# Sparse attention and a token mixer on one core: batch 0's theta and first mix half in plain float32, mixing weights split later, batch 0's scores from copied keys, and a new order

## The chip, the cores and the metric

The kernel runs on one core of a Trainium2 chip. The metric is the device time of one execution in microseconds (us), as the median of several runs. One further execution was recorded by the hardware profiler; durations come from that record.

The engines are named as in the profile: PE (TensorE, matrix products), PEld (its weight loads), DVE (VectorE), ACT (ScalarE), POOL (GpSimd) and SP (SyncE, which here issues all DMAs). Each engine works off its own list of instructions in a fixed order and waits where an operand is not there yet.

## The reference

Attention with a window and block sums, then a mixer over tokens and channels. Cut to what matters:

```python
# attention: B, H, S, D = 4, 8, 768, 64; block 32, window 16
k_sum = k.reshape(B, H, 24, 32, D).max(axis=3)
v_sum = v.reshape(B, H, 24, 32, D).mean(axis=3)
scores = concat(where(|i - j| < 16, q @ k.T / 8, -1e9), q @ k_sum.T / 8 + log(32))
x = softmax(scores) @ concat(v, v_sum)        # laid out as (B, S, 512)
# mixer
theta = x @ w_theta                           # 512 x 512
zr, zi = x * cos(theta), x * sin(theta)
u = x + w_tok_r @ zr + w_tok_i @ zi           # 768 x 768, over tokens
out = u + relu(u @ w_ch)                      # 512 x 512
```

The four mixer weights come to the device as float64-like 8-byte words and are turned into float32 there.

## The kernel before

**Tiles.** A batch has 768 tokens, in six tiles of 128; the whole run has 24 tiles. A tile goes through these steps, and the name in brackets is that of the step in the planner's tables:

- `att_tile` (KV, S, SM, AV): load queries and values, scores (L598, 118 keys for each group of 64 queries: 24 block maxima and 94 neighbours), masked minimum (L619, DVE), exponential (L623, ACT), transposes on PE (L632) with a copy out (L636), product with the values (L606), division (L651 on ACT or L653 on DVE).
- `turn_tile` (X): transpose the result `xn` on PE (L662). From it come `x` (kept for the sum), and the split into a rounded part `xh` and a rest `xl` (L446, L448 and L667).
- `theta_tile` (TH, Z): theta on PE (L686), range reduction (L694, L697, L698, L703), sine and cosine (ACT, L709 and L710, with table loads between exponential and sine), products with `xn` (L718), one for each half of the channels: the first half goes into `w`, the second into `zb`.
- `split_z` makes `zh` and `zl` of a half of the channels.
- `mix_step(b, h, s)` (M0, M1): for batch b, half h of the channels and token tile s, 4 groups of 6 products on PE (L739) into PSUM tiles `m`. After six steps a half is complete; `x` is added to it on DVE (L754) and it is sent to DRAM.

At the end the last matrix product (`out_unit`, L787) runs for all batches.

**Split products.** A product with full precision is made of three passes of the type float32r: rounded weight by rounded data, rest of the weight by rounded data, rounded weight by the rest of the data. So weights and data are split into a rounded part and a rest.

**Weights.** `load_f64` handles one block of a weight: four blocks of theta (`wth`, 128 x 512), twelve of the token mixer (`wt`, 128 x 768) and at the end four of the last product. Its steps are the DMA, the magnitude (L492 on ACT or L494 on DVE), clamp (L496), shift (L498), two assembling operations (L500, L502), the rounded part (L446 on ACT, L448 on DVE) and the rest (L455 on DVE or POOL). The split block takes the place of the 8-byte words in the same buffer. All sixteen blocks pass through here in the first 90 us of a run.

**Keys.** In batch 0 (`DIRECT=1` counts batches) the scores read the block maxima `ks` and the keys `kn` directly, as two products each. In the other batches ACT or POOL copy both into one tile `k` (L591), which has one buffer, and there is one product of 118 columns.

**Order.** Nothing runs in the order of the source. `Program` collects all operations with a cost for each engine that may take them, and plans the order of every engine ahead, with four rounds of forward and backward passes and a last pass in which the tables `OFF` (a shift of rank) and `HOLD` (an earliest time) for each step act. The emitted lists are fixed; on the chip only semaphores hold an instruction back.

## Time and profile before

| | |
|---|---|
| median of 3 runs | 486.13 us (486.02 to 486.48) |
| the profiled execution: its time, its span | 486.1 us, 484.3 us |
| instructions | 10093 |
| DMA | 62.13 MB, 128 GB/s over the span |
| PE, time busy in the first 108 us | 72.5 us |
| DVE, time busy from 12 to 96 us | 81.1 of 84 us |
| ACT, time busy from 24 to 120 us | 85.1 of 96 us |

The span runs from the first to the last instruction; 1.8 us of the execution's time lie around it. A row of a timeline gives the start, the length, the engine, the line, the operation, the tile written and those read, and a count where like rows are merged. Rows of one engine overlap by some hundredths of a microsecond, and by more on PE, where products are pipelined; so the spacing of starts is the price there, and the mean length is not. One float32 product (not float32r) appears as two PE records.

### The profile page before, as it was taken

The page shows a single profiled execution, that of the slowest core. Times are in us where ns is not written, and L with a number is a line of the kernel's source. Part 1 is how long each engine was busy: PE and PEld are TensorE (multiplying, and loading weights), DVE is VectorE, ACT ScalarE, POOL GpSimd, SP SyncE. Part 2 cuts the span into 40 slices and gives each one's busy share as a digit, 9 for nine tenths or more (in the row PEclk, how much of TensorE's full clock was granted, in tenths as well). Part 3 has the DMA queues.
Part 4 walks back from the last instruction along what each step waited for, and adds up shares of the span by engine and source line. Part 5 has one row for each costly group of instructions (what it writes and reads, how often), then busy time and mean ns, then how long its engine had stood idle before and what let it go on. Part 6 is the DMA issues. An engine that isn't in the chain of part 4 may idle for free.

```text
span 484.3 us, 10093 instructions
## 1 busy us (share of the span) xinstructions
PE 444.8 (92%) x3864; PEld 378.1 (78%) x3864; DVE 301.6 (62%) x871; ACT 302.3 (62%) x663; POOL 51.6 (11%) x85
## 2 busy tenths in 40 slices
PE   0856676899999999999999999999999999999997
PEld 0344555778888878888888888888888899999996
DVE  3999999987784755476665745542645691334343
ACT  1678979799987776678896879536644640031120
POOL 0003111410200010011021110101000100001010
PEclk9979799899999999999999999999999999999999
DMA  8996824454461341013511411020012440256553
GB/s 306 364 345 200 325 76 172 140 164 136 121 214 56 100 143 33 1 56 122 191 56 56 142 37 55 7 94 1 0 67 88 152 132 0 99 162 213 196 180 130
DMA packets 30768, 62.13 MB, mean 128 GB/s; under 512 B 3584, under 2 KB 14080, under 8 KB 30720
## 3 DMA queue, kind: packets, MB, share of 16 engines
q1 hardware_dynamic: 30720, 61.49, 38.6%
q8 instruction: 30, 0.49, 0.4%
q14 instruction: 18, 0.15, 0.1%
HBM read 48.90 MB, written 12.58 MB: 127 GB/s over the span
## 4 chain that ended last, share of the span: by engine, by line
PE 74%; DVE 14%; ACT 7%; issue 2%; DMA 2%; SPq 0%; POOL 0%; ACTq 0%; POOLq 0%
PE m L739 36%; PE c L787 14%; PE t L686 12%; PE pa L606 4%; PE pa L632 4%; PE s L598 3%; DVE f L500 2%; DVE f L502 2%; PE t L662 2%; DMA kn<-kT 2%; DVE wt L455 1%; ACT e L623 1%; ACT L709 1%; DVE f L496 1%; DVE ks L522 1%
## 5 line engine op out<-in xcount | busy, mean ns | idle before, releaser
L739 PE MATMUL m<-wt,zh 128*128 128x512 f32 (+1 forms) x768 | 169.5, 342 | 1.7 <-ACT zh L446 1.7
L739 PEld LDWEIGHTS m<-wt,zh 128*128 128x128 f32 x768 | 121.1, 189 | 20.6 <-ACT zh L446 2.1
L739 PE MATMUL m<-wt,zl 128*128 128x512 f32 (+1 forms) x384 | 99.1, 339 | 0.7 <-DVE zl L455 0.7
L686 PE MATMUL t<-wth,xh 128*128 128x512 f32 x192 | 66.8, 430 | 8.0 <-DVE xl L667 6.7
L739 PEld LDWEIGHTS m<-wt,zl 128*128 128x128 f32 x384 | 58.6, 188 | 9.3 <-DVE zl L455 1.0
L787 PE MATMUL c<-cuh,wth 128*128 128x384 f32 x256 | 65.2, 335 | 0.0
L623 ACT ACTIVATE e<-e,st 128x118 f32<-128x118 f32 x192 | 60.1, 386 | 5.1 <-DVE st L619 4.9
L619 DVE CUSTOM_DVE_ANT_0 e<-s,cs 128x118 f32<-128x118 f32 x192 | 42.2, 273 | 20.1 <-PE s L598 15.8
L446 ACT CAST cuh<-cu 128x384 fp32r<-128x384 f32 x32 | 16.0, 513 | 60.2 <-DMA cu<-u_scratch 60.1
L787 PEld LDWEIGHTS c<-cuh,wth 128*128 128x128 f32 x256 | 45.8, 188 | 0.4
L792 DVE SCALAR_TENSOR_TENSOR cu<-c,cu 128x384 f32<-128x384 f32 x32 | 17.1, 554 | 43.6 <-PE c L787 43.5
L686 PEld LDWEIGHTS t<-wth,xh 128*128 128x128 f32 x192 | 31.4, 196 | 14.9 <-DVE xl L667 8.1
L787 PE MATMUL c<-cul,wth 128*128 128x384 f32 x128 | 43.0, 336 | 0.0
L686 PE MATMUL t<-wth,xl 128*128 128x512 f32 x96 | 39.4, 410 | 0.0
L697 DVE TENSOR_SCALAR w<-w 128x512 f32<-128x512 f32 x19 | 8.1, 426 | 46.0 <-ACT w L694 46.0
L632 PE MATMUL pa<-cs,e 128*118 128x128 f32 x192 | 29.7, 281 | 6.7 <-ACT xn L651 5.2
L636 ACT COPY e<-pa 118x512 f32<-118x512 f32 x45 | 25.2, 584 | 13.3 <-PE pa L632 13.3
L632 PEld LDWEIGHTS pa<-cs,e 128*118 128x118 f32 x192 | 23.1, 139 | 12.7 <-ACT xn L651 6.3
L606 PEld LDWEIGHTS pa<-v,e 118*64 118x64 f32 x768 | 24.6, 137 | 9.2 <-ACT e L636 5.3
L694 ACT ACTIVATE w<-t,bmagic 128x512 f32<-128x512 f32 x24 | 16.5, 687 | 24.1 <-PE t L686 23.6
L606 PE MATMUL pa<-v,e 118*64 118x65 f32 x768 | 28.2, 224 | 3.6 <-ACT e L636 3.6
L591 POOL COPY k<-kn 128x188 f32<-128x188 f32 x40 | 14.6, 392 | 118.2 <-PE s L598 98.8
(81 smaller groups left out, 657.3 us busy)
## 6 DMA issues: line engine op xcount, KB each, us to landing
v<-vg SPq DMA_DIRECT2D x48, 195.0 KB, 2.9
q<-qg SPq DMA_DIRECT2D x24, 256.0 KB, 3.4
cu<-u_scratch SPq DMA_DIRECT2D x32, 192.0 KB, 3.0
out<-cu SPq DMA_DIRECT2D x32, 192.0 KB, 1.9
kn<-kT SPq DMA_DIRECT2D x6, 798.0 KB, 6.5
wt<-wtr SPq DMA_DIRECT2D x6, 768.0 KB, 10.8
wt<-wti SPq DMA_DIRECT2D x6, 768.0 KB, 9.8
f<-vT SPq DMA_DIRECT2D x12, 384.0 KB, 3.2
```

The costliest lines, as they stand in the source:

```text
L446: nc.scalar.copy(dst(), src())
L591: lambda e, dst=dst, src=src: (nc.scalar.copy if e == "ACT" else V[e].tensor_copy)(dst(), src()), rd, [(k, key)], due, port=BOTH)
L606: mm(2 * 0.433, [lambda n=n, g=g, a=a: nc.tensor.matmul(xa[a].get()[ROW[g], n], turned[a].get()[:NK, n * P + g * QT:n * P + (g + 1) * QT], ...
L619: op({"DVE": 0.205}, lambda eng, n=n: nc.vector.tensor_tensor_reduce(e()[:, n], sc[n % 2].get()[:, 2 * a + n // 2], mask(m), -SCALE, 3.0e3 ...
L623: op({"ACT": 0.288}, lambda eng, n=n: nc.scalar.activation(e()[:, n], e()[:, n], AF.Exp, bias=st.get()[:, n:n + 1], scale=-1.0), [(st, n)] ...
L632: mm(NH * 0.109, [lambda n=n: nc.tensor.transpose(tp.get()[:NK, n], e()[:, n], ident()) for n in range(NH)], [e_ref, (cs, "ident")], [tp], ...
L636: lambda e: (nc.scalar.copy if e == "ACT" else nc.vector.tensor_copy)(t.get()[:NK], tp.get()[:NK].rearrange("k n q -> k (n q)")), [tp], [t ...
L686: calls = [lambda t=t, xx=xx, k=k, c=c: nc.tensor.matmul(th.get(), xx.get()[:, c], w_th[c].get()[:, k], start=(c == 0 and t == 0), stop=(c ...
L694: op({"ACT": 0.59}, lambda e: nc.scalar.activation(r(), th.get(), AF.Identity, bias=bmagic.get(), scale=1.0 / TWO_PI), [th, bmagic], [R], due)
L739: nc.tensor.matmul(acc[th](), zz.get()[:, r, cc], w_t[s, r].get()[:, k, TT[th]], start=(s == 0 and r == 0 and t == 0 and (th == 0 or c == 0)),
L787: calls = [lambda t=t, k=k, uu=uu, c=c, co=co, acc=acc: nc.tensor.matmul(acc.get(), w_ch[c].get()[:, k, co * P:(co + 1) * P], uu.get()[:, ...
L792: op({"DVE": c_dve(HT)}, lambda e, co=co, acc=acc: nc.vector.scalar_tensor_tensor(u.get()[:, co], acc.get(), 0.0, u.get()[:, co], ALU.max, ...
```

## The change

The diff of the tables is of no use to a reader: `OFF` and `HOLD` are replaced as a whole, and the three numbers of the planner's last pass with them. What it does to the order is shown below. The rest, cut to its core:

```diff
+def c_raw(n):
+    return n * 1.675e-3
...
-            A1=13, T1=10, PREP=5, QB=2, VSPE=1, VB=4, KN=2, DIRECT=1, XA=6, ...
+            A1=13, T1=10, PREP=5, QB=2, VSPE=1, VB=4, KN=2, DIRECT=0, RT=6, RM=6, XA=6, ...
...
-        op({"ACT": c_act(n), "DVE": c_dve(n)}, magnitude, [raw], [f_ref], due)
+        op({"ACT": c_act(n), "DVE": c_dve(n, "fast")}, magnitude, [raw], [f_ref], due, port=BOTH)
...
-        hi_op(lambda: w.get()[:, 0], f, n, [f_ref], [(w, 0)], due)
-        lo_op(lambda: w.get()[:, 1], f, lambda: w.get()[:, 0], n, [f_ref, (w, 0)], [(w, 1)], due)
+        return (to, f_ref if into is None else key)
+
+    def split_f64(j, tag, whole, n, due, pool=wpool, bufs=1):
+        pr.late, pr.key = K["R_W2"], ("W2", j)
+        src, key = whole
+        w = tag if isinstance(tag, Ref) else Ref(pool, [P, 2, n], F32R, tag=tag, bufs=bufs)
+        hi_op(lambda: w.get()[:, 0], src, n, [key], [(w, 0)], due, engines=("ACT", "DVE", "POOL"))
+        lo_op(lambda: w.get()[:, 1], src, lambda: w.get()[:, 0], n, [key, (w, 0)], [(w, 1)], due)
         return w
...
-        if b < K["DIRECT"]:
+        if b * NT + i < K["DIRECT"]:
...
+        if b * NT + i >= K["RT"]:
             x_h = Ref(tpool, [P, NC, P], F32R, tag="xh", bufs=K["XHB"])
             x_l = Ref(tpool, [P, NC, P], F32R, tag="xl", bufs=K["XHB"])
...
+            if b * NT + i < K["RT"]:
+                mm(c_raw(DM), [lambda c=c: nc.tensor.matmul(
+                    th.get(), xt[b].get()[:, c, i * P:(i + 1) * P], f_th[c][0](), start=(c == 0), stop=(c == NC - 1))],
+                   [(xt[b], i), f_th[c][1]], [th], due)
+                continue
...
-        split_z(b, 0, i, w, lambda: w.get()[:, :, :HC], due)
+        if not raw:
+            split_z(b, 0, i, w, lambda: w.get()[:, :, :HC], due)
+        else:
+            zs[b, 0, i] = z_0, None
...
+                if z_l is None:
+                    terms = ((z_h, f_t[2 * s + r][0]()),)
+                else:
+                    terms = [(zz, w_t[s, r].get()[:, k]) for zz, k in ((z_h, 0), (z_h, 1), (z_l, 0))]
...
+    def split_wt(j, f):
+        if len(slots) >= 2 * NT and f[1] and f[1][0] is slots[-2 * NT]:
+            f_ref = Ref(apool, [P, S], tag="f", bufs=K["FB"])
+            hi_op(f_ref.get, f[0], S, [f[1]], [f_ref], 1e6, engines=("ACT", "DVE", "POOL"))
+            f = f_ref.get, f_ref
+        w_t[j // 2, j % 2] = split_f64(NC + j, slot([P, 2, S], F32R), f, S, 1e6)
...
         mix_step(b, h, s, m_time(t))
+        if t < K["RM"]:
+            for j in (2 * s, 2 * s + 1):
+                split_wt(j, f_t[j])
```

In words:

- `RT=6`: theta of tiles 0 to 5 is one float32 product for each of its four blocks, of the unsplit `x` and the unsplit weight, in the place of three float32r products. `xh` and `xl` are not made for these tiles. The unsplit theta weights lie in the buffers of `xh` and `xl`.
  The split theta blocks, needed from tile 6 on, are made in the new order while the mixing blocks are assembled: two of the four subtractions on DVE, two on POOL.
- `RM=6`: the six steps of batch 0's first half (M0) take the unsplit product `zh` and the unsplit mixing weight, one float32 product where there were three. `zl` is not made for them.
- The twelve mixing blocks share one ring of twelve buffers. A block is split (rounded part, rest) after it has been assembled, under a rank of its own (W2). The rounded part may go to POOL too. One block, whose own buffer is the one to be written, is first copied. The DMA of the twelfth block waits for the buffer of the first.
- `DIRECT=0`: batch 0's scores use copied keys as the other batches do.

**Three places in the order.** Tile names carry a number where they would be mistaken otherwise. On DVE, the seventh and eighth mixing block of before (`f` is the float32 block in the making, `wt` the 8-byte words and later the split block, `e`, `st` belong to the scores):

```order
L498 TENSOR_SCALAR f<-f 128x768
L500 SCALAR_TENSOR_TENSOR f<-wt_629,f 128x768
L500 SCALAR_TENSOR_TENSOR f<-wt_613,f 128x768
L502 SCALAR_TENSOR_TENSOR f<-wt_629,f 128x768
L502 SCALAR_TENSOR_TENSOR f<-wt_613,f 128x768
L697 TENSOR_SCALAR w<-w 128x512
L455 TENSOR_TENSOR wt_759<-f,wt_759 128x768
L455 TENSOR_TENSOR wt_770<-f,wt_770 128x768
```

And on DVE in the change, where two blocks and then tile 0's product for the first half are made:

```order
L505 TENSOR_SCALAR f<-f 128x768
L509 SCALAR_TENSOR_TENSOR f<-wt,f 128x768
L507 TENSOR_SCALAR f<-f 128x768
L512 SCALAR_TENSOR_TENSOR wt<-wt,f 128x768
L509 SCALAR_TENSOR_TENSOR f<-wt,f 128x768
L512 SCALAR_TENSOR_TENSOR wt<-wt,f 128x768
L745 TENSOR_TENSOR zh<-xn,w 128x512
```

The subtraction for the rest of the block has left this place, and the product is written straight to `zh`, without `zl` behind it. The first such subtraction for a mixing block now stands on DVE behind all twelve blocks.

On PE, the first mix step, before (`m` is the sum in PSUM, `t` theta, `pa` the product with the values):

```order
L686 MATMUL t<-wth_327,xh 128x512 x2
L686 MATMUL t<-wth_327,xl 128x512
L606 MATMUL pa_730<-v,e 64x65 x8
L606 MATMUL pa_739<-v,e 64x65 x8
L739 MATMUL m_761<-wt_353,zh 128x512
L739 MATMUL m_763<-wt_353,zh 128x256
L739 MATMUL m_761<-wt_353,zh 128x512
L739 MATMUL m_763<-wt_353,zh 128x256
L739 MATMUL m_761<-wt_353,zl 128x512
L739 MATMUL m_763<-wt_353,zl 128x256
```

And in the change (`xh` and `xl` here name the buffers of theta's unsplit weights):

```order
L706 MATMUL t<-xh,x 128x512
L706 MATMUL t<-xl,x 128x512
L651 MATMUL pa_576<-cs,e 118x128 x4
L706 MATMUL t<-xh,x 128x512
L706 MATMUL t<-xl,x 128x512
L773 MATMUL m_596<-wt,zh 128x512
L773 MATMUL m_598<-wt,zh 128x256
L773 MATMUL m_596<-wt,zh 128x512
L773 MATMUL m_598<-wt,zh 128x256
```

A block of a step is now two products for each of real and imaginary part, and the step stands before the products of a fourth tile with its values, where it stood behind them.

On ACT, the head of the list, before and then in the change:

```order
L492 ACTIVATE f<-wth_95 128x512
L446 CAST wth_127<-f 128x512
L446 CAST wth_171<-f 128x512
L623 ACTIVATE e<-e,st 128x118 x8
L551 ACTIVATE vs<-pa_110 24x8x64
```

```order
L610 COPY k<-ks 128x8x24
L610 COPY k<-kn 128x2x94 x3
L642 ACTIVATE e<-e,st 128x118 x6
L501 ACTIVATE f<-wth_104 128x512
L569 ACTIVATE vs<-pa_108 24x8x64
```

The key copies of tile 0 now come first, and the scores of the tile stand ahead of the theta weights.

More of the change, by code (lines that the diff above doesn't have):

```diff
@@ L161 @@
     ROUNDS = 4
-    LAST = (dict(PE=0, ACT=0.4648, DVE=1.1037, POOL=0.8482, SP=0), 8.4091, 0.404)
+    LAST = (dict(PE=0, ACT=0.5052, DVE=1.0781, POOL=1.0202, SP=0), 6.4848, -1.0921)
     LOAD = 1.283
@@ L447, in fn @@
             else:
-                nc.vector.tensor_copy(dst(), src())
-        cost = {"ACT": c_act(n, psum), "DVE": c_dve(n, "psum" if psum else "fast")}
+                V[e].tensor_copy(dst(), src())
+        cost = {"ACT": c_act(n, psum), "DVE": c_dve(n, "psum" if psum else "fast"), "POOL": c_pool(n, False)}
         op({e: cost[e] for e in engines}, fn, reads, writes, due, port=() if psum else BOTH)
@@ L813, in theta @@
             n = done[1]
+            if n == K["RT"] > 0:
+                for c in range(NC):
+                    w_th.append(split_f64(c, f"wth{c}", f_th[c], DM, 1e6))
             turn_tile(n // NT, n % NT, 1e6)
@@ L819, in attn_moe, with slot, land @@
     for c in range(NC):
-        w_th.append(load_f64(f"wth{c}", wth[c], DM, wpool, apool, 1e6))
-    for s in range(NT):
-        for r in range(2):
-            w_t[s, r] = load_f64(f"wt{s}{r}", (wtr, wti)[r][s], S, wpool, apool, 1e6)
+        raw = load_f64(c, f"wth{c}", wth[c], DM, 1e6)
+        if K["RT"]:
+            to = Ref(tpool, [P, DM], tag=("xh", "xl")[c % 2], bufs=K["XHB"])
+            f_th.append(to_f32(c, raw, DM, apool, 1e6, to.get, to))
+        else:
+            w_th.append(split_f64(c, f"wth{c}", to_f32(c, raw, DM, apool, 1e6), DM, 1e6))
+    slots = []
+    def slot(shape, dtype):
+        slots.append(Ref(wpool, shape, dtype, tag="wt", bufs=2 * NT))
+        return slots[-1]
+    landed = []
+    def land(j):
+        pr.late, pr.key = K["R_W"], ("W", NC + j)
+        raw = slot([P, 2 * S], I32)
+        dma(raw.get, lambda: (wtr, wti)[j % 2][j // 2], S * 1024, [], [raw], 1e6, 6144)
+        landed.append(raw)
+    def split_wt(j, f):
+        if len(slots) >= 2 * NT and f[1] and f[1][0] is slots[-2 * NT]:
+            f_ref = Ref(apool, [P, S], tag="f", bufs=K["FB"])
+            pr.late, pr.key = K["R_W2"], ("W2", NC + j)
+            hi_op(f_ref.get, f[0], S, [f[1]], [f_ref], 1e6, engines=("ACT", "DVE", "POOL"))
+            f = f_ref.get, f_ref
+        w_t[j // 2, j % 2] = split_f64(NC + j, slot([P, 2, S], F32R), f, S, 1e6)
+    first = 2 * NT - 1 if K["RM"] else 2 * NT
+    for j in range(first):
+        land(j)
+    for j in range(2 * NT):
+        if j < 2 * K["RM"]:
+            if j % 2 == 0:
+                two = slot([P, 2, S], F32)
+            f_t.append(to_f32(NC + j, landed[j], S, apool, 1e6, lambda two=two, j=j: two.get()[:, j % 2], (two, j % 2)))
+            if j == 1:
+                land(2 * NT - 1)
+        else:
+            f, f_ref = to_f32(NC + j, landed[j], S, apool, 1e6)
+            split_wt(j, (f, (f_ref, None)))
     attend(2)
```

73 lines of the change are left out of this document (42 added, 31 removed), and 116 rows, old and new, of tables (HOLD, OFF).

## The prediction

> **What bounds the kernel now.** I read the shares of the page first, then the busy times by stretch.
>
> ```profile
> span 484.3 us, 10093 instructions
> PE 444.8 (92%) x3864; PEld 378.1 (78%) x3864; DVE 301.6 (62%) x871; ACT 302.3 (62%) x663; POOL 51.6 (11%) x85
> ```
>
> ```profile
> 12.00:24.00 12.00, 10.05 (x147) 4.37 (x145) 10.91 (x35) 7.28 (x17) 0.00 (x0) 1.00 1.04 363
> 60.00:72.00 12.00, 8.49 (x115) 7.01 (x116) 11.68 (x30) 9.57 (x21) 1.66 (x2) 1.00 0.25 68
> 84.00:96.00 12.00, 9.95 (x72) 8.15 (x73) 11.89 (x30) 8.92 (x24) 5.74 (x11) 0.86 0.47 144
> 108.00:120.00 12.00, 12.00 (x167) 9.91 (x167) 8.95 (x33) 11.66 (x25) 0.69 (x2) 1.00 0.50 144
> 120.00:160.00 40.00, 40.00 (x396) 33.52 (x392) 27.96 (x105) 34.35 (x90) 4.61 (x8) 1.00 0.41 128
> ```
>
> The columns behind the length are PE, PEld, DVE, ACT, POOL, the granted clock, the DMA share and GB/s. Until 96 us DVE has no free time while PE is idle for a sixth to a third of it; from 108 us PE is full and DVE is not. The chain of waits changes hands in the same place:
>
> ```profile
> 62.70 1.74 DVE f L502 x2
> 64.77 1.75 DVE wt L455 x2
> ...
> 82.60 0.95 DVE f L502
> ...
> 98.33 0.97 PE t L686 x3
> ...
> 120.44 1.26 PE m L739 x6
> ...
> 128.53 0.44 PE pa L632 x4
> 128.96 1.05 PE m L739 x6
> ```
>
> It follows the making of weights until some 90 us and PE products behind that. The last row ends batch 0's first mix half, at 130.0 us: call that **the mark**. The span is the time of the mark plus PE's work behind it, and both are worked out below.
>
> **PE's prices.** From the chain, the price of float32r products and of scores from copied keys; from the timeline, a plain float32 product and scores read directly:
>
> ```profile
> 130.01 1.08 PE pa L606 x32
> ...
> 144.45 0.71 PE t L686 x3
> 146.29 0.97 PE s L598 x32
> ...
> 372.98 15.89 PE m L739 x90
> ```
>
> ```profile
> 15.76 3.61 PE L528 MATMUL pa<-x,vt 128*24 128x512 f32 x8
> 69.21 0.31 PE L598 MATMUL s<-ks,q 64*64 64x24 f32 x8
> ...
> 70.48 0.73 PE L686 MATMUL t<-wth,xh 128*128 128x512 f32 x2
> ```
>
> ```profile
> L739 PEld LDWEIGHTS m<-wt,zh 128*128 128x128 f32 x768 | 121.1, 189 | 20.6 <-ACT zh L446 2.1
> ```
>
> - A mix group (six products, 2304 columns) takes 1.05 us, so 512 float32r columns take 0.233. Three theta products take 0.70.
> - Eight records of L528 are four float32 products. They take 3.61 us with a tail of about 0.16 for the last, so 0.43 a record, **0.866 for 512 columns** and 0.433 for 256. The stationary side has 24 columns there and will have 128. A load of 128 float32r columns takes 189 ns and lies beside the product before it, of which the shortest record would be 217 ns; so I add nothing, and keep four full float32r passes (4 x 0.233 = 0.933) as the upper end.
> - A raw mix group takes 1.30 us, 0.25 more; 24 groups add 6.0. A raw theta block adds 0.166; 24 add 4.0.
> - Direct scores of a tile take 1.27 (69.21 to 70.48), copied ones 0.97. Six tiles save 1.9 with the first, colder ones.
>
> That is 10.0 - 1.9 = **8.1 us more PE work**. Counted along the two orders, both have 24 mix groups, ten tiles' scores and eight tiles' products with values ahead of the mark; the change has eight transposes fewer there (four of them take 0.44 us in the chain) and one theta block of tile 6 more (0.70). So 7.9 of the 8.1 lie ahead of the mark, and PE's work behind it stays the same to 0.2 us. **The span moves as the mark moves**, as long as PE stays full afterwards.
>
> A rule of the skill speaks against this: by the Trainium skill, "FP8 and Floating Point Precision", section "TensorE Precision Notes", true float32 takes four passes through the array. The L528 row comes to 0.866/0.233 = 3.7 float32r passes; at four whole ones PE would have 12.1 us more instead of 8.1.
>
> **DVE up to the mix steps.** The last two of twelve blocks are assembled at 83.5 us:
>
> ```profile
> 79.99 1.82 DVE L500 SCALAR_TENSOR_TENSOR f<-wt,f 128x768 int32<-128x768 int32 x2
> 81.73 1.82 DVE L502 SCALAR_TENSOR_TENSOR f<-wt,f 128x768 uint32<-128x768 uint32 x2
> ```
>
> ```profile
> L455 DVE TENSOR_TENSOR wt<-f,wt 128x768 fp32r<-128x768 f32 x9 | 8.5, 962 | 0.3 <-ACT wt L446 0.3
> L448 DVE CAST wt<-f 128x768 fp32r<-128x768 f32 x2 | 1.1, 556 | 0.0
> L455 DVE TENSOR_TENSOR wth<-f,wth 128x512 fp32r<-128x512 f32 x8 | 5.4, 680 | 0.7 <-ACT wth L446 0.7
> L667 DVE TENSOR_TENSOR xl<-t,xh 128x512 fp32r<-128x512 f32 x24 | 16.5, 687 | 3.4 <-ACT x L446 2.7 <-ACT xh L446 0.4
> L496 DVE TENSOR_SCALAR f<-f 128x768 f32<-128x768 f32 x7 | 3.9, 552 | 0.0
> ```
>
> Up to the last assembly DVE's two lists hold the same scores (five tiles) and the same blocks. Gone from the change's are: eight rests of mixing blocks (8 x 0.962 = 7.7), two roundings of them (1.1), two of the four rests of theta blocks (1.4), three `xl` (2.1) and two `zl` (1.4 at the same size): 13.7. It has three more clamps of 768 columns (1.7) and smaller rows that come to 0.5 less. That makes **12.5 us** of rows. Rows overlap: the pair above starts 1.74 apart for 1.90 of length, a factor of 0.92; so 11.5 us. Against it stands the head: eight score rows (1.6 us) now come ahead of the first weight, and wait for a mask that lands behind more loads; no row shows this; from the keys' loads, which now lead, it could be 0.5 us earlier, and with the whole wait on DVE's idle list 2.4 later. I take 0.8 later, nearer to the present row. The twelfth block is then assembled at 83.5 - 11.5 + 0.8 = 72.8.
>
> Tile 2's `zh`, which mix step 2 waits for, stands 3.6 us of rows behind that on DVE (six score rows, one key maximum, the product itself), at 76.1. PE goes on from there with four mix steps (16 x 1.30 = 20.8), eight raw theta blocks (6.9), tile 6's four (2.8), four tiles' scores (3.9), three with values (3 x 1.08), 40 transposes of 0.11: 42.0 us. Between 120.44 and the mark the chain takes 9.57 us for rows of 9.2 by these prices, since a change of kind costs something: 4% more. 76.3 + 43.5 = **119.8**.
>
> A second way goes by ACT, which is nearly full (11.66 of 12 us in the stretch from 108):
>
> ```profile
> 76.44 1.75 ACT L492 ACTIVATE f<-wt 128x768 f32<-128x768 f32 x2
> 119.61 0.61 ACT L710 ACTIVATE w<-w 128x512 f32<-128x512 f32 x1
> ```
>
> ```profile
> L446 ACT CAST zh<-w 128x512 fp32r<-128x512 f32 x19 | 11.7, 618 | 5.1 <-PE m L739 3.9 <-DVE w L718 1.0
> L446 ACT CAST wt<-f 128x768 fp32r<-128x768 f32 x10 | 8.2, 829 | 4.0 <-DVE f L502 3.9
> L446 ACT CAST xh<-t 128x512 fp32r<-128x512 f32 x11 | 6.4, 579 | 0.0
> ```
>
> From the last magnitude (78.2) to tile 5's second sine (120.2) ACT takes 42.0 us, and its rows between the two sum to the same in the change within 0.5: the `zh`, `xh` and weight roundings that go are made up by key copies and by later splits that come in. The last magnitude should end 5 (as now) to 9 us ahead of 72.8, so the sine at 106 to 110, and the mark 9.8 + 1.0 later (four groups are raw): 117 to 121. Both ways agree.
>
> I take 119.8 and 0.7 for a wait more: mark at 120.5, **9.5 us earlier**. Span 484.3 - 9.5 = 474.8. The profiled execution took 486.1 with 1.8 us around the span, and the median is 486.13, so 486.1 - 9.5 = **476.6 us**.
>
> What is moved and hidden: the twelve rests and roundings of mixing blocks now fall between some 80 and 120 us. They are 12 x 0.962 = 11.5 us if DVE does all rests, and 12 x 0.829 = 9.9 of roundings on ACT (POOL may take some of both). DVE has 12 us free in 120 to 160, and the second half begins with two blocks only. Without that room its end, and the time, would come up to 11.5 us later. DVE's first addition into `x` at the mark waits for PE, as before; queued behind it are four rests, tile 6's second product and a tile's scores, needed by the second half some microseconds later. On SP the twelfth block's load waits for the first block's buffer, freed when the first two are assembled; behind it are queries and values of the last tiles of batch 0. By the list of issues a block is 768 KB:
>
> ```profile
> wt<-wtr SPq DMA_DIRECT2D x6, 768.0 KB, 10.8
> ```
>
> Eleven are 8.7 MB, and with keys, queries and values about 17 MB stand ahead of it: 47 us at the 363 GB/s of the first stretch. By the counting above the buffer is free at 37, so nothing waits.
>
> **The rivals.**
>
> - *Keys in one buffer.* All six tiles of batch 0 now wait for four copies, which wait for the tile before to have used the buffer. In batches 1 to 3 this costs nothing, as the group shows:
>
> ```profile
> L598 PE MATMUL s<-k,q 64*64 64x118 f32 x576 | 18.7, 267 | 0.2 <-DMA f<-vT 0.2
> L591 ACT COPY k<-kn 128x188 f32<-128x188 f32 x32 | 9.6, 347 | 5.1 <-PE s L598 5.0
> L492 ACT ACTIVATE f<-wt 128x768 f32<-128x768 f32 x12 | 10.9, 920 | 1.1 <-DVE wt L455 1.1
> ```
>
>   But there PE has other work, and ahead of 60 us it has little. A chain of four copies on ACT behind one magnitude is 4 x 0.35 + 0.92 = 2.3 us a tile, 13.9 for six: the mark at 134.4, **490.5 us, slower**. It decides from 1.6 us a tile. Against it: POOL is idle early and takes ten of these copies, and DVE, not PE, is late there.
> - *Four full passes.* If a float32 product with 128 stationary columns takes four float32r passes, 0.933, PE has 2.1 us more from step 2 to the mark and 1.9 before, which count as soon as PE is late: up to 4.0 more, **480 us**. For it speaks that no row has such a product; against it the 0.43 of a record. The page of the Trainium skill named above, "FP8 and Floating Point Precision", would have it so.
> - *Nothing gained.* The wait only goes from DVE to ACT: if ACT's last magnitude stays at 78 us, the mark comes at 78.2 + 42.0 + 10.8 = 131 and the time is **487 us**, within 0.2% or just above. Against it: ACT loses ten roundings of 0.83 in the same stretch.
> - *No wait left.* By the same counting tile 0's `zh` is there at 51.3, and from its step to the mark PE has 65.2 us of work, 67.8 with the 4%: the mark at 119.1. So even a PE that is full from there gains only 1.4 us more: **475 us**, unless DVE runs ahead.
>
> **How the numbers follow.** Forecast and "no wait left" together 0.72, four passes 0.12, keys 0.11, nothing gained 0.05. A measurement of this kernel can tell about 0.2% (1 us) from no change. Faster by more: 0.84; within: 0.04; slower: 0.12 ("nothing gained" gives 0.04 to the one and 0.01 to the other). The predicted time is 476.6. The range goes from 471.5 (DVE's start at its early end, 1.3; no further wait, 0.7; and the 2.9 us that DVE idles now between 12 and 96 gone) to 483 (the start at its late end, 1.6; four full passes, 4.0; a microsecond of new waits), which leaves out "keys" and "nothing gained".
>
> **What would show it.** In the changed profile: L706 records 0.43 apart and groups of four L773 records in 1.30 us; L512 for the twelfth block ending at 71 to 75 us; the first L773 near 51, where the first L739 is at 60.8 now:
>
> ```profile
> 60.82 0.96 PE L739 MATMUL m<-wt,zh 128*128 128x512 f32 x4
> ```
>
> the first addition row of batch 0 shortly before 120, and PE full from there. Wrong would be: idle time of PE ahead of L617 put down to key copies; a mark behind 126; PE idle behind it.

## The result, and the profile after

| | before | after |
|---|---|---|
| median | 486.31 us | **480.66 us** |
| single executions | 486.02 to 486.49 us | 478.79, 480.64, 480.68, 480.69 us |
| ratio to before | | **0.9875 (95% interval 0.9851 to 0.9899)** |
| profiled execution: time, span | 486.1, 484.3 us | 478.79, 477.0 us |

The change makes the kernel 1.25% faster. The forecast was 476.6 us (471.5 to 483.0): the sign and the range hold, and the forecast itself is 4.1 us too low. The profiled execution happens to be the fastest of the four; the others have a span of 478.9 us. The first experiment profiles an execution of this longer kind and shows where such a difference lies.

First the head of the page of the changed kernel:

```profile
span 477.0 us, 9565 instructions
PE 451.1 (95%) x3600; PEld 366.8 (77%) x3600; DVE 310.1 (65%) x880; ACT 292.3 (61%) x656; POOL 43.5 (9%) x83
```

PE is 6.3 us busier than before (451.1 against 444.8), yet the span is 7.3 us shorter: PE idles 25.9 us instead of 39.5. So the gain is PE idle time that went (13.6 us), minus PE work that came (6.3 us).

The busy times by stretch, with the columns as before:

```profile
84.00:96.00 12.00, 11.66 (x101) 6.78 (x100) 9.78 (x34) 10.19 (x20) 1.36 (x3) 1.00 0.30 91
108.00:120.00 12.00, 12.00 (x104) 8.23 (x103) 8.51 (x29) 10.60 (x20) 2.60 (x6) 1.00 0.21 61
```

From 84 us on PE is nearly full, where before it was idle for 2.05 of 12 us; from 108 us it is full, as before.

The chain of waits of the changed kernel, at the places that answer to the rows shown of before (start, length, engine, tile, line):

```profile
75.48 0.85 DVE wt L512
...
79.30 0.60 DVE zh L745
...
122.57 1.49 PE m L773 x4
```

The twelfth block is assembled at 76.4 us (83.5 before; forecast 72.8). Tile 2's `zh` starts at 79.2, and the mark, the end of batch 0's first mix half, stands at 124.1 us (130.0 before; forecast 120.5).

The prices of PE's new products stand in its timeline:

```profile
62.40 1.02 PE L706 MATMUL t<-xh,x 128*128 128x512 f32 x2
63.26 1.02 PE L706 MATMUL t<-xl,x 128*128 128x512 f32 x2
...
65.18 5.43 PE L773 MATMUL m<-wt,zh 128*128 128x512 f32 x16
```

Two raw theta blocks start 0.86 us apart. Four raw mix groups (16 records) take 5.43 us; without the tail of the last record, 0.16 by the prediction's own row, that is 1.32 each. These are the prices of the forecast (0.866 and 1.30) within 2%.

### The profile page after: what moved, and what is told of

The parts are those of the page before. It is cut to its first block, busy times and chain, and to the rows that moved or that the text cites. A ratio compares the mean times of both kernels' runs of the same rounds, so it can differ in the third digit from the quotient of the medians.

```text
span 477.0 us, 9565 instructions
## 1 busy us (share of the span) xinstructions
PE 451.1 (95%) x3600; PEld 366.8 (77%) x3600; DVE 310.1 (65%) x880; ACT 292.3 (61%) x656; POOL 43.5 (9%) x83
## 4 chain that ended last, share of the span: by engine, by line
PE 82%; DVE 9%; DMA 6%; issue 1%; SPq 1%; ACT 0%; ACTq 0%
PE m L773 40%; PE c L825 14%; PE t L711 11%; PE pa L625 5%; PE s L617 4%; PE pa L651 3%; DMA v<-vg 2%; DMA wt<-wtr 2%; PE t L681 2%; DVE f L509 2%; DVE wt L512 2%; PE t L706 2%; DMA x<-vn 1%; DVE e L638 1%; DVE f L507 1%
## 5 line engine op out<-in xcount | busy, mean ns | idle before, releaser
L773 PE MATMUL m<-wt,zh 128*128 128x512 f32 (+1 forms) x768 | 181.5, 360 | 1.9 <-DVE zh L745 1.9
L773 PEld LDWEIGHTS m<-wt,zh 128*128 128x128 f32 x768 | 123.4, 189 | 32.8 <-issue 12.6
L773 PE MATMUL m<-wt,zl 128*128 128x512 f32 x336 | 86.7, 339 | 0.0
L773 PEld LDWEIGHTS m<-wt,zl 128*128 128x128 f32 x336 | 51.4, 188 | 7.3
L711 PE MATMUL t<-wth,xh 128*128 128x512 f32 x144 | 48.1, 415 | 0.1
L638 DVE CUSTOM_DVE_ANT_0 e<-s,cs 128x118 f32<-128x118 f32 x192 | 42.6, 273 | 7.1 <-PE s L617 3.3
L722 DVE TENSOR_SCALAR w<-w 128x512 f32<-128x512 f32 x18 | 7.7, 430 | 50.1 <-ACT w L719 50.1
L655 ACT COPY e<-pa 118x512 f32<-118x512 f32 x45 | 25.6, 585 | 14.8 <-PE pa L651 14.7
L610 POOL COPY k<-kn 128x188 f32<-128x188 f32 x48 | 16.9, 383 | 131.3 <-PE s L617 118.1
L711 PE MATMUL t<-wth,xl 128*128 128x512 f32 x72 | 28.4, 394 | 0.0
L617 PE MATMUL s<-k,q 64*64 64x118 f32 x768 | 26.7, 279 | 1.2 <-ACT e L642 1.2
## 6 DMA issues: line engine op xcount, KB each, us to landing
wt<-wtr SPq DMA_DIRECT2D x6, 768.0 KB, 11.1
wt<-wti SPq DMA_DIRECT2D x6, 768.0 KB, 12.6
```

Source lines behind the costliest of these rows:

```text
L610: lambda e, dst=dst, src=src: (nc.scalar.copy if e == "ACT" else V[e].tensor_copy)(dst(), src()), rd, [(k, key)], due, port=BOTH)
L617: mm(0.79 if len(parts) == 1 else 2.1, [lambda p=p, g=g, h=h, c=c, kk=kk: nc.tensor.matmul(sc[h].get()[ROW[g], p, c], q.get()[ROW[h], p, R ...
L638: op({"DVE": 0.205}, lambda eng, n=n: nc.vector.tensor_tensor_reduce(e()[:, n], sc[n % 2].get()[:, 2 * a + n // 2], mask(m), -SCALE, 3.0e3 ...
L655: lambda e: (nc.scalar.copy if e == "ACT" else nc.vector.tensor_copy)(t.get()[:NK], tp.get()[:NK].rearrange("k n q -> k (n q)")), [tp], [t ...
L711: calls = [lambda t=t, xx=xx, k=k, c=c: nc.tensor.matmul(th.get(), xx.get()[:, c], w_th[c].get()[:, k], start=(c == 0 and t == 0), stop=(c ...
L773: nc.tensor.matmul(acc[th](), zz.get()[:, r, cc], w[:, TT[th]], start=(s == 0 and r == 0 and t == 0 and (th == 0 or c == 0)), stop=(s == N ...
```

## The experiments

In most of them the order of the changed kernel is kept and single operations are moved. `move(ns, before)` takes operations out of the planned list by their place in it and puts them ahead of another one. Of each kernel, the table gives the start of VectorE's first weight row (L503; L494 in the kernel before), the end of the twelfth block (last row of L512 on 768 columns), the mark (the first addition row, L792, that waits for PE), and the span, all from the profiled execution, and the median and ratio of the timed ones.

| kernel | first weight row | twelfth block | mark | span | span less mark | median | ratio to before |
|---|---|---|---|---|---|---|---|
| before | 11.44 | 83.55 | 130.05 | 484.3 | 354.3 | 486.3 | |
| changed | 15.24 | 76.44 | 124.09 | 477.0 | 352.9 | 480.66 | 0.9875 (0.9851 to 0.9899) |
| r1_repeat | 16.48 | 78.29 | 125.92 | 479.5 | 353.6 | 481.88 | 0.9898 (0.9870 to 0.9926) |
| r2_weight_first | 11.67 | 77.57 | 125.20 | 478.4 | 353.2 | 480.52 | 0.9869 (0.9847 to 0.9891) |
| r3_pool_later | 15.41 | 75.74 | 124.72 | 478.6 | 353.9 | 480.84 | 0.9877 (0.9857 to 0.9897) |
| r4_pool_load | 16.09 | 87.78 | 135.43 | 489.1 | 353.7 | 490.19 | 1.0067 (1.0049 to 1.0085) |
| r5_warm | 15.18 | 76.09 | 124.21 | 476.9 | 352.7 | 478.74 | 0.9843 (0.9810 to 0.9875) |
| r6_reduce_later | 16.15 | 77.88 | 125.62 | 478.3 | 352.7 | 479.68 | 0.9848 (0.9826 to 0.9870) |
| r7_direct | 16.56 | 78.60 | 126.25 | 479.0 | 352.8 | 481.24 | 0.9885 (0.9863 to 0.9906) |
| r12_all | 11.54 | 75.39 | 122.81 | 475.7 | 352.9 | 477.72 | 0.9821 (0.9804 to 0.9838) |

Two differences carry the reading of the whole case. Span less mark is 352.7 to 353.9 us in all rows behind the first, so what happens ahead of the mark decides the time. And in these rows the mark stands 47.4 to 48.1 us behind the twelfth block, but for r3 (49.0), though the block itself moves over 12 us.

### The same kernel again

No edit.

> The changed kernel again, unchanged. The profiled run of it had a span of 477.0 us at a mean clock of 0.982, its other runs 478.9 at 0.978. If the 1.9 us more are one more stretch of low clock on TensorE ahead of the mark (which ends at 124.0 us in the profile), a profile at the longer level has its mark near 125.9 and 353 us behind it. If they lie in the full stretch behind, the mark stays at 124.0 and 355 us follow. A time near 480.7 either way.

Measured: 480.51 to 482.88 us, profiled at 481.27. Here is PE at the start of the first profile and then of this one:

```profile
9.23 3.35 PE L546 MATMUL pa<-x,vt 128*24 128x512 f32 x4 [9.23 <-DMA x<-vn]
12.52 1.04 PE L617 MATMUL s<-k,q 64*64 64x118 f32 x32
```

```profile
9.44 3.58 PE L546 MATMUL pa<-x,vt 128*24 128x512 f32 x4 [9.44 <-DMA x<-vn]
12.95 1.85 PE L617 MATMUL s<-k,q 64*64 64x118 f32 x32
```

Both start with half of the product of values (L546) at about half speed. In one the scores of tile 0 behind it run at 1.04 us, in the other at 1.85. VectorE waits for these scores, and its list of minima and weight rows starts 1.25 us later:

```profile
13.63 0.28 DVE L638 CUSTOM_DVE_ANT_0 e<-s,cs 128x118 f32<-128x118 f32 x1 [2.46 <-PE s L617]
```

```profile
14.88 0.28 DVE L638 CUSTOM_DVE_ANT_0 e<-s,cs 128x118 f32<-128x118 f32 x1 [3.57 <-PE s L617]
```

Nothing gives it back: set row against row, this execution is 1.25 us behind the first at 14 us, 1.85 at the twelfth block, 1.83 at the mark and 2.5 at the end. So most of the longer level of the changed kernel is made ahead of the mark, and half of it in the first 15 us.

The clock that the trace records goes with it. Its first record of full speed starts at 12.23 us in the first profile, ahead of the scores, and at 14.84 in r1, where they end at 14.80. Six of the profiled kernels start with these same rows and no products ahead of them: in two (the first profile and r3) that record starts at 12.2 and 12.6 us and the scores take 1.04, in four (r1, r2, r4, r6) it starts at 14.2 to 14.8 and they take 1.71 to 1.85.

By the Trainium skill, "TensorE: Matmul & The Clock Gate", section "What's actually happening", the window in which the array's activity is counted is free-running, so the point where products become fast varies from run to run with the phase at the start; the two rows of L617 agree with that.

### Weights ahead of tile 0's scores

```diff
     order = pr.schedule()
...
+    move([56, 57, 58], 34)
```

> The first three weight rows on VectorE (magnitude, clamp and shift of theta block 1, 1.35 us) stand ahead of tile 0's eight score rows, in the time in which VectorE idles (2.5 us ahead of 13.63 us); nothing else moves. Theory 'late head' (the first weight row at 15.24 us instead of some 13.5 is part of why the mark is late, and VectorE carries it through): first weight row near 12.1 us, the twelfth block 1.3 to 1.6 earlier (near 75.0), the mark near 122.5, time 1.3 to 1.6 below the unchanged kernel's 480.7. Rival 'no matter' (VectorE's start is made up by a wait later on): twelfth block and mark within 0.4 us of 76.4 and 124.0, time 480.7.

Measured: the first weight row at 11.67 us, as its data land. In this profile tile 0's scores took 1.73 us on PE, the slow kind, so it stands against r1: the twelfth block is 0.7 us earlier, the mark 0.7, the span 1.1, the median 1.4. "Late head" holds by the rows; the intervals of the two ratios overlap. The gain is about half of what the rows moved (1.35 us), and below the 1.3 to 1.6 expected. Tile 0's minima, and with them ScalarE's first exponentials, come only 0.2 us earlier (14.68 against 14.88); that this is the reason is not shown.

### GpSimd's split moved away from VectorE's last blocks

VectorE and GpSimd between 66 and 74 us in the changed kernel:

```profile
66.33 0.96 DVE L507 TENSOR_SCALAR f<-f 128x768 int32<-128x768 int32 x1
67.21 1.08 DVE L512 SCALAR_TENSOR_TENSOR wt<-wt,f 128x768 uint32<-128x768 uint32 x1
68.22 1.09 DVE L509 SCALAR_TENSOR_TENSOR f<-wt,f 128x768 int32<-128x768 int32 x1
...
70.03 0.68 DVE L723 CUSTOM_DVE_ANT_0 w<-t,w 128x512 f32<-128x512 f32 x1
70.63 1.12 DVE L512 SCALAR_TENSOR_TENSOR wt<-wt,f 128x768 uint32<-128x768 uint32 x1
...
72.48 1.50 DVE L745 TENSOR_TENSOR zb<-xn,w 128x512 f32<-128x512 f32 x1
73.90 0.55 DVE L507 TENSOR_SCALAR f<-f 128x768 int32<-128x768 int32 x1
```

```profile
65.59 1.28 POOL L722 TENSOR_SCALAR w<-w 128x512 f32<-128x512 f32 x1 [22.33 <-DVE f L505]
66.94 1.56 POOL L610 COPY k<-kn 128x188 f32<-128x188 f32 x2
...
70.12 0.82 POOL L454 CAST wt<-wt 128x768 fp32r<-128x768 f32 x1
71.03 2.40 POOL L461 TENSOR_TENSOR wt<-wt 128x768 fp32r<-128x768 f32 x1
```

L507 takes 0.55 us alone (73.90) and 0.96 beside GpSimd's L722 and the copy behind it; L745 takes 1.50 beside the subtraction L461. L723, which reads PSUM, keeps its 0.68.

```diff
     order = pr.schedule()
...
+    move([364], 407)
+    move([366], 460)
```

> The rounding and the rest of the first mixing block, which GpSimd does at 70.1 to 73.4 us beside VectorE's last weight rows, are issued later on GpSimd (rounding ahead of the second block's rounding, rest ahead of the third's). Theory 'stretched rows' (a VectorE row that reads and writes SBUF alone takes longer while GpSimd works): the rows of L512 and L745 near 71 to 73 us go back from 1.12 and 1.50 to 0.95 and 0.69 us, the twelfth block near 75.4, the mark near 123.0, time about 1 us below the unchanged kernel's. Rival 'other cause' (PSUM, DMA or order): these rows keep 1.1 and 1.5 us, and the time stays.

Measured, in the rows that the theory names:

```profile
70.93 0.94 DVE L512 SCALAR_TENSOR_TENSOR wt<-wt,f 128x768 uint32<-128x768 uint32 x1
72.60 0.68 DVE L745 TENSOR_TENSOR zb<-xn,w 128x512 f32<-128x512 f32 x1
```

Both are back at their own length. The head of this profile is of the faster kind (first weight row 15.41), so it stands against the first profile: the twelfth block is 0.7 us earlier in spite of a head 0.2 later. But the mark is 0.6 later. The moved subtraction now runs at 95.5 us, in a stretch in which PE is full and hangs on VectorE's next `xn`. Ahead of that `xn` VectorE makes a rounding (L454), and this row takes 2.84 us there; it takes 1.06 in the changed kernel (second view), and 0.55 alone (at 100.79 us there):

```profile
94.83 2.84 DVE L454 CAST wt<-wt 128x768 fp32r<-128x768 f32 x1
...
95.46 1.80 POOL L461 TENSOR_TENSOR wt<-wt 128x768 fp32r<-128x768 f32 x1
```

```profile
95.51 1.06 DVE L454 CAST wt<-wt 128x768 fp32r<-128x768 f32 x1
```

And PE in r3:

```profile
100.31 0.77 PE L681 MATMUL t<-cs,xn 128*128 128x128 f32 x4 [0.99 <-DVE xn L672]
```

PE waits 0.99 us there, a wait that the changed kernel doesn't have. The theory of the rows holds, and the forecast of the time (1 us less) fails: at its new place the same instruction stretches another row of VectorE, and there it costs more.

### More work on GpSimd

```diff
...
+    spare = lambda: zs[0, 1, 0][1].get().rearrange("p a n -> p (a n)")[:, :480]
+    for n in (232, 234, 237, 239, 243, 245, 247, 249, 253, 258, 264, 270):
+        extra = Op()
+        extra.eng = "POOL"
+        extra.fn = lambda e: nc.gpsimd.tensor_tensor(spare(), cs.get()[:, 0:480], cs.get()[:, 2:482], op=ALU.subtract)
+        order.insert(order.index(first[n]), extra)
```

> Twelve subtractions of 480 columns on GpSimd with no use, into a buffer that is not used so early, behind its rest of theta block 0 (from 43.3 us on, some 14 to 19 us in all); VectorE makes weights there. Theory 'stretched rows': by the overlapped rows of the changed kernel (L509 1.33 instead of 0.95 us at 0.74 us of overlap, so 0.5 us for each us beside GpSimd) and with two thirds of VectorE's rows there on SBUF alone, VectorE loses 4 to 6 us; the twelfth block near 81, the mark near 129, time 485 to 487. Rival 'other cause': VectorE's rows keep their lengths, time 480.7.

Measured: 490.19 us, above even the kernel before. VectorE's groups between 44 and 62 us, first in this kernel and then in the changed one (line, engine, operation, tiles, shapes, count, busy us, mean ns, idle us ahead):

```profile
L512 DVE SCALAR_TENSOR_TENSOR wt<-wt,f 128x768 uint32<-128x768 uint32 x4 | 6.4, 1625 | 0.0
...
L505 DVE TENSOR_SCALAR f<-f 128x768 f32<-128x768 f32 x2 | 2.7, 1336 | 0.0
...
L745 DVE TENSOR_TENSOR zh<-xn,w 128x512 f32<-128x512 f32 x1 | 1.5, 1468 | 0.0
L638 DVE CUSTOM_DVE_ANT_0 e<-s,cs 128x118 f32<-128x118 f32 x4 | 0.9, 268 | 0.0
```

```profile
...
L512 DVE SCALAR_TENSOR_TENSOR wt<-wt,f 128x768 uint32<-128x768 uint32 x6 | 5.5, 949 | 0.0
L505 DVE TENSOR_SCALAR f<-f 128x768 f32<-128x768 f32 x6 | 3.3, 556 | 0.1
...
L638 DVE CUSTOM_DVE_ANT_0 e<-s,cs 128x118 f32<-128x118 f32 x4 | 0.9, 268 | 0.0
```

Rows that work on SBUF alone take 1.7 to 2.4 times as long; L638, which reads PSUM, doesn't move. L745, left out of the second view, takes 0.68 there. GpSimd's twelve took 17.75 us in all. Against r1 the twelfth block is 9.5 us later, the mark 9.5 and the span 9.6: more than the 4 to 6 us expected. The row that the expectation names, L509 at 1.33 us, stands in no profile; in the first profile of the changed kernel the rows of L509 on 768 columns beside GpSimd take 1.09 and 1.93. "Stretched rows" holds, "other cause" is out, and this is at the same time the plainest sign that VectorE carries the mark one to one.

By the Trainium skill, "SBUF — State Buffer", section "Who interferes with whom", VectorE and GpSimd share a pair of ports under an exclusive lock; a VectorE instruction with two SBUF inputs, or a copy, cast or `tensor_scalar` in a two-port mode, contends with GpSimd, one that reads SBUF once at the plain rate doesn't. Which rows stretch here (L505, L507, L512, L745) and which don't (L638, L723) agrees with it.

### TensorE warmed ahead of its first product

```diff
...
+    zero, to = zb[0, 0], macc[0, 0][0]
+    def warm(src, before):
+        extra = Op()
+        extra.eng = "PE"
+        extra.fn = lambda e: nc.tensor.matmul(to.get()[:, :256], zero.get()[:, 0, :P], src(), start=True, stop=True)
+        order.insert(order.index(first[before]), extra)
...
+    for n in range(6):
+        warm(lambda: zero.get()[:, 1], 20)
+    for half, count in ((0, 2), (1, 3)):
+        for n in range(count):
+            warm(lambda half=half: keys[0][half].get()[:, 1 - half, :256], 20)
```

> Eleven float32 products of 256 columns with no use stand on TensorE ahead of the first product with values: six on zeros from about 1 us, two and three behind the second and third load of keys; GpSimd clears the zeros first. The order of all else is the same. Theory 'cold start' (the first four records of the value product take 3.4 to 3.6 us where the next eight take 3.6, and tile 0's scores behind them 1.04 in one profile and 1.85 in another, so TensorE starts slow and VectorE's first scores and weights wait for it): these four records take 1.75 to 1.9 us, the scores 1.04 and start near 11.6, the first weight row starts near 13.8 instead of 15.24 to 16.48, everything behind it moves by as much, time 479.0 or below, 1.5 to 2.5 less than the unchanged kernel's median. Rival 'no matter': the scores come earlier and the first zh of tile 2 doesn't, time 480.7 to 481.9.

Measured: 478.74 us.

```profile
9.41 1.90 PE L546 MATMUL pa<-x,vt 128*24 128x512 f32 x4
11.70 1.04 PE L617 MATMUL s<-k,q 64*64 64x118 f32 x32 [0.39 <-issue]
```

```profile
13.57 0.28 DVE L638 CUSTOM_DVE_ANT_0 e<-s,cs 128x118 f32<-128x118 f32 x1 [2.36 <-DMA cs<-cst]
```

The product of values takes 1.90 us, the scores 1.04, ending at 12.74: PE's part came out as expected. The first weight row did not come at 13.8 but at 15.18, for a new wait stands in the place of the old one: the mask (`cs`), whose load lands at 13.44. Even so the head is 1.3 us earlier than in r1, the mark 1.7, the span 2.6 and the median 3.1 (2.7 by the ratios to before).

It differs little from the first profile of the changed kernel. There the scores ended at 13.56 and the mask had landed at 13.38, so the mask alone would have held VectorE nearly as long. In r1 the mask landed at 13.50 and the scores ended at 14.80: only there do the slow products set the head. Three of r5's four executions are at 478.2 to 478.8 and one is at 481.4; that the warming makes the short scores the usual case fits these times, but one profile does not show it.

### VectorE's key maxima behind tile 2's zh

```diff
...
+    move([365, 379], 410)
+    move([389], 427)
```

> The two key maxima of batch 1 (1.75 us each), which stand on VectorE ahead of and behind tile 2's zh, come 15 rows later, behind tile 3's angles, and ScalarE's copy of them with them. Theory 'VectorE carries the mark' (the mark comes 44 us after tile 2's zh): zh some 1.1 us earlier (its second sine ends at 78.0, it started at 79.22), the mark and the time 1.1 us earlier, up to 2 with the second maximum. Rival 'ScalarE carries it': zh comes earlier, but tile 3's and 4's sines do not, PE idles more between 80 and 92 us, mark and time within 0.4 us of the unchanged kernel's.

Measured: `zh` 1.6 us earlier than in r1, the mark 0.3, the median 479.68. In the profile it now waits 0.41 us for ScalarE's sine, and PE, which waited 0.45 us for `zh` in r1, does so no more. PE waits for the last two sums of values of batch 1 instead:

```profile
79.50 0.69 DVE L745 TENSOR_TENSOR zh<-xn,w 128x512 f32<-128x512 f32 x1 [0.41 <-ACT w L735]
```

```profile
PE pa L566 <- DVE vt L562: 0.8, 2, 0.6
```

The data of these sums had landed at 85.0 and 87.2 us. On VectorE they stand behind the two moved maxima:

```profile
85.31 3.40 DVE L540 TENSOR_REDUCE ks<-kn 128x48 f32<-128x1536 f32 x2
...
89.50 1.81 DVE L562 TENSOR_REDUCE vt<-f 128x24 f32<-128x768 f32 x2
```

So what is won at `zh` is lost on VectorE again, at the place to which the maxima went. The mark gains no more than the head of this profile, but not for the rival's reason: that ScalarE carries the mark is not shown here. Of the 1.2 us less in span, 0.3 come with the head of this profile and 0.9 behind the mark; whether those belong to the edit is open, and the intervals of the two ratios touch.

### Keys read directly

```diff
+        near = b * NT + i < 5
+        if near:
+            for o in pr.ops[-4:]:
+                o.fn = lambda e: None
+            parts = ((slice(0, NB), lambda p, g, r: ks.get()[r, p]),
+                     (slice(NB, NK), lambda p, g, r: kn[p // 2].get()[r, p % 2, (2 * i + g) * QT:(2 * i + g) * QT + NL]))
...
```

> Tiles 0 to 4 of batch 0 read their keys directly, 16 more products a tile; their 20 local copies (10 on ScalarE, 10 on GpSimd or near it) are left out, the order is the same otherwise. The prediction's step (copied keys save 0.3 us of TensorE a tile, more at the low clock, and no wait): 1.5 us of TensorE more in five tiles, of which little counts ahead of 72 us as VectorE is late there, time 0 to 1.5 us above the unchanged kernel's. Rival 'the copies cost a wait' (tiles wait for copies in one buffer): scores come earlier, time 1 us or more below.

Measured: 481.24 us against 481.88 and 480.66 for the changed kernel, no difference that can be told. Twelfth block and mark are 0.3 us later than r1's, the end 0.5 earlier. Copied keys were neither a wait nor a gain that these runs can tell.

### Without the tables of the order, and with one half of the change at a time

The change also brings new tables. In these four `OFF` and `HOLD` are empty, so the planner's own order stands; in two of them one half of the change is undone as well.

```diff
-OFF = {
...
-HOLD = {
...
+OFF, HOLD = {}, {}
```

In r10 the number of tiles with plain theta goes to 0, in r11 that of plain mix steps:

```diff
-DIRECT=0, RT=6, RM=6
+DIRECT=0, RT=0, RM=6
```

```diff
-DIRECT=0, RT=6, RM=6
+DIRECT=0, RT=6, RM=0
```

> The changed kernel with both tables of the order (OFF and HOLD) empty: the planner's own order. Theory 'work' (the gain is the work that leaves VectorE): against the kernel before with empty tables it keeps a gain of 1 to 2%. Rival 'search' (the gain is the newly searched order): without tables the two are equal within 0.3% or the changed one is slower. Either is some 2 to 5% slower than with its tables.

> The kernel before with both tables empty, the other half of that comparison: 'work' says 5 to 10 us slower than the changed kernel without tables, 'search' says within 1.5 us of it or faster.

> The changed kernel without tables, batch 0's theta split again (three float32r products, weights and x split early), the mix half plain. By the prediction's rows VectorE has 3.5 us more ahead of the twelfth block, TensorE 4.0 us less: theory 'VectorE carries the mark' says 2 to 4 us above the changed kernel without tables. Rival 'TensorE carries it': 2 to 4 us below.

> The changed kernel without tables, batch 0's mix half split again, theta plain. By the prediction's rows VectorE has 10.3 us more ahead of the twelfth block (eight rests, two roundings, two zl), TensorE 6.0 us less: 'VectorE carries the mark' says 5 to 9 us above the changed kernel without tables. 'TensorE carries it': 4 to 6 us below.

| without tables | median | ratio to before (with its tables) | twelfth block | span | PE idle in the span |
|---|---|---|---|---|---|
| r9, before | 496.15 | 1.0205 (1.0177 to 1.0233) | 89.55 | 494.7 | 44.2 |
| r11, theta plain, mix split | 493.52 | 1.0138 (1.0121 to 1.0155) | 87.73 | 492.3 | 41.6 |
| r10, theta split, mix plain | 490.18 | 1.0071 (1.0052 to 1.0089) | 80.94 | 487.8 | 36.6 |
| r8, the changed kernel | 488.32 | 1.0033 (1.0018 to 1.0048) | 78.47 | 487.2 | 31.1 |

The idle time is the span less PE's busy time on the page of each, here r9, r11, r10 and r8 in turn:

```profile
PE 450.5 (91%) x3864; PEld 382.0 (77%) x3864; DVE 299.7 (61%) x853; ACT 304.7 (62%) x672; POOL 60.4 (12%) x100
```

```profile
PE 450.7 (92%) x3648; PEld 372.0 (76%) x3648; DVE 303.0 (62%) x874; ACT 299.2 (61%) x656; POOL 48.9 (10%) x93
```

```profile
PE 451.2 (92%) x3624; PEld 374.2 (77%) x3624; DVE 309.5 (63%) x872; ACT 298.4 (61%) x665; POOL 57.9 (12%) x92
```

```profile
PE 456.1 (94%) x3600; PEld 367.4 (75%) x3600; DVE 303.7 (62%) x869; ACT 296.3 (61%) x661; POOL 53.1 (11%) x88
```

Without tables the change is worth 7.8 us (496.15 to 488.32), with them 5.7. So the gain is the work and does not hang on the searched tables (each kernel keeps its own three numbers of the planner's last pass). The new tables are worth 7.7 us to the changed kernel, the old ones 9.8 to the kernel before. The plain mix half carries most of it (5.2 us of time, 10.5 of idle time against 5.4 of added work); plain theta adds 1.9, just under the 2 to 4 expected. "TensorE carries it", by which r10 and r11 would have been faster than r8, is out.

The twelfth block comes in the same order as the time. Plain theta brings it 2.5 us forward (r10 to r8; 3.5 by the prediction's rows), the plain mix half 9.3 (r11 to r8; 10.3 by the rows), the whole change 11.1. So the rows that leave VectorE do what the prediction says. The time moves by less (1.9, 5.2 and 7.8 us). The mark can't be compared in these orders, since each puts other work ahead of it: it is at 137.3 us in r8 and at 136.1 in r9, and in the first 137 us PE is busy for 110.2 us in r8 and 97.4 in r9.

### Several pieces together

```diff
...
+    move([13], 12)
+    move([56, 57], 34)
+    move([365], 416)
+    move([379], 422)
+    move([389], 432)
+    move([410], 527)
+    move([364], 407)
+    move([366], 555)
+    move([460], 464)
+    first[460].eng = "DVE"
```

and the warming products of r5.

> The changed kernel with the useful pieces together: the eleven warming products on TensorE; the mask's load ahead of the second load of values (with the warming alone VectorE then waited 2.4 us for the mask); two weight rows ahead of tile 0's scores; GpSimd's first mixing rounding and rest and VectorE's key maxima of batch 1 later, a rest behind them too; GpSimd's third mixing rounding on VectorE. Theory 'VectorE carries the mark': head 2 us earlier than with the warming alone or 3 ahead of the unchanged kernel, another 1 us from the rows that no longer stretch, the mark near 120 to 121.5, time 476.5 to 478. Rival 'ScalarE or a load takes over' (tile 2's second sine, the vT loads): the head comes earlier and the mark doesn't, time 478.5 to 480.

Measured: 477.72 us (477.07 to 479.48), below both kernels; the interval of its ratio overlaps that of the warming alone (r5). The mark is at 122.8, later than the 120 to 121.5 expected. Two terms failed. This time the third load of keys landed later (7.7 us, 7.0 in r5), PE idled 1.9 us between the warming products, and the rest of them ran slow, so that tile 0's scores ended at 14.7 though the mask had landed at 12.0:

```profile
7.78 4.11 PE L945 MATMUL m<-kn,zb 128*128 128x256 f32 x10 [1.91 <-DMA kn<-kT]
```

And tile 2's `zh` waited 1.04 us for ScalarE's sine, the rival's mechanism:

```profile
77.92 0.69 DVE L745 TENSOR_TENSOR zh<-xn,w 128x512 f32<-128x512 f32 x1 [1.04 <-ACT w L735]
```

## Why the prediction was right, and where it was not

**"The span moves as the mark moves" held.** The mark came 6.0 us earlier in the profile, the span 7.3. PE's work behind the mark, forecast as unchanged to 0.2 us, took 1.4 us less (354.3 to 352.9; 0.7 less in r1). Of this 0.9 is busy time (350.3 to 349.4) and 0.5 idle time. By the records the same products run there, but for six transposes more and one theta block less, as forecast to about that (eight and one); why they take less was not looked into.

**PE's prices held.** A record of a float32 product takes 0.43 us, a raw theta block 0.86, a raw mix group 1.32. "Four full passes" would have had 0.93 and 1.40, so that rival is out: a float32 product costs 0.86/0.233 = 3.7 float32r passes at 128 stationary columns too. The rule of the Trainium skill that the prediction cites, "FP8 and Floating Point Precision", section "TensorE Precision Notes", is about the number of passes. No row here counts passes, so what failed is the price of 0.233 for each of them, and the rule stays open.

Ahead of the mark, where the prediction put 7.9 of its 8.1 us more PE work, PE's busy time grew by 7.2 (94.5 to 101.75). These times also hold products at the low clock (granted 0.64 in the stretch from 24 to 36 us, 0.72 before), so the difference isn't resolved. The 1.9 us credited to copied keys could not be seen at the end (r7). That VectorE's lateness would have swallowed this PE time is likely, but no run shows it.

**From the twelfth block to the mark the sum was right.** Forecast 47.7 us (72.8 to 120.5), measured 47.65, and 47.4 to 48.1 in all but one of the kernels that keep the order. From tile 2's step to the mark it was 43.5 forecast and 44.1 measured (79.96 to 124.06). By the prediction's own terms that part is 42.0 and 4%, 43.7, from 76.1 on and not 43.5 from 76.3; the sum is the same. PE idled 0.24 us between the two, and the hidden rests and roundings stayed hidden.

**The step that failed is the time of the twelfth block, "72.8".** It came at 76.4, and at 78.3 in r1, which stands for the usual execution. The term of 12.5 us of rows that leave VectorE was not at fault; two other terms were.

- *The head, "0.8 later".* VectorE's list of minima and weights began 2.2 us later than in the kernel before (11.44 to 13.63) in the profile, and 3.4 later (14.88) in r1. The prediction had the wait for the mask in view, bounded the head at 2.4 late and took 0.8. In the profile the mask, landed at 13.38, makes some 2 us of the 2.2 by itself: a term that was seen and sized too small. In r1 the slow products add 1.3 us, and these the prediction did not see: tile 0's scores stand on PE behind half of the product of values, which runs at half speed at the start of the program, and the scores themselves run at either speed. This term makes 1.4 us of the error, 2.6 in the usual execution.
- *Rows beside GpSimd.* The prediction took VectorE's rows at the lengths of before. There none up to the twelfth block is longer than its like by more than 0.07 us; GpSimd's two subtractions (37.7 and 46.1 us) stand beside score rows. In the change eight rows are longer. Five of the rows shown between 66 and 74 us are longer by 0.13 to 0.82 than their own lengths (0.55, 0.95, 0.95, 0.95, 0.68): 1.7 us in all. Three rows at 26.7, 40.7 and 42.2 us add 1.5; the last of them takes 1.93 instead of 0.95, beside a rest of theta on GpSimd:

```profile
42.15 1.93 DVE L509 SCALAR_TENSOR_TENSOR f<-wt,f 128x768 int32<-128x768 int32 x1
```

```profile
42.00 1.26 POOL L461 TENSOR_TENSOR wth<-xh,wth 128x512 fp32r<-128x512 f32 x1 [0.73 <-ACT wth L452]
```

r3 gets two of the eight back, and r4 shows the mechanism at full size.

From the list's start to the twelfth block VectorE took 72.1 us before and 62.8 in the change, 9.3 less where 11.5 were forecast. The 3.2 us of longer rows, against 1.2 us less of waits within the list (2.8 to 1.6), make 2.0 of these 2.2. In r1 it is 3.3 and 0.8 of 2.8. What made the waits fewer, and the rest of 0.2 to 0.3, no run took apart.

**The sum of the error.** Profiled: block 3.6 late, behind the mark 1.4 early, span 2.2 above the 474.8 forecast. Usual execution (r1): 5.5 late, 0.7 early, 4.7 above. The median stands between, 4.1 above. That the range held is in part luck: 4.0 us of its late end were for four full passes, which did not come, it had no term for longer rows, and in r1 the head is a microsecond beyond its bound.

**The signs.** The prices of L706 and L773 came as named. The first L773 (53.7 us, named near 51), the twelfth block (76.4, named 71 to 75) and the first addition row (122.4, named shortly before 120) came late. Of the signs of being wrong none came, though r1's mark, 125.9, is just short of the 126 named.

**The rivals.** "Keys in one buffer" did not occur: by the page PE idles 1.2 us in all ahead of L617, for an exponential and not for keys, and r7 gains nothing. "Nothing gained" is out. "No wait left" is out as well, since PE still idles ahead of 96 us. The rival of the second half of the experiments, ScalarE, may be next: in r6 and r12 tile 2's `zh` waits 0.4 and 1.0 us for its sine, and in r12 the chain of waits lies on ScalarE from 69.1 to 85.5 us. No run makes ScalarE faster, so this is not shown.

## What to carry to other kernels

Look for the instruction that starts the bounding engine's list, and follow what it waits for through the other engines' queues: here VectorE's list waited for the load of the mask and for scores behind a product with no hurry that ran at half speed, and 1.25 us there (r1) came out as 1.8 at the mark. Where the bounding engine works on SBUF alone, look at what GpSimd does beside it: twelve subtractions with no use cost 9.5 us, and one that was only moved (r3) cost more at its new place. And sum a trade of work between engines by idle time: 6.3 us more on PE were paid for by 13.6 us less waiting.
